# The first loads and a whole instruction order, in a kernel of sparse attention and a gated feed-forward layer

## The chip, the cores and the metric

One core of a Trainium2 chip. A core has five engines that run beside each other, each through its own instructions in order: TensorE (PE, matrix products; its weight loads are PEld), VectorE (DVE), ScalarE (ACT), GpSimd (POOL) and SyncE (SP), which here only issues transfers. ScalarE and GpSimd issue some too. Transfers run on 16 DMA engines that all queues share. The metric is the time of one execution on the device in microseconds (us); a profiled execution gives the time of every instruction.

## The reference

Attention over 4 batches of 8 heads, 768 positions of 64 values, with a mask by blocks of 32 (neighbours, the first and last block, three drawn blocks a row), and then a feed-forward layer with gate `h * sigmoid(beta * h)`:

```python
scores = scale * np.matmul(q, k.transpose(0, 1, 3, 2))
...
scores = np.where(mask, scores, -1000000000.0)
scores = scores - np.max(scores, axis=-1, keepdims=True)
attn = np.exp(scores)
attn = attn / (np.sum(attn, axis=-1, keepdims=True) + 1e-09)
...
h = x @ w_in                                  # 3072 x 512 by 512 x 2048
g = h * (1.0 / (1.0 + np.exp(-beta * h)))
return (g @ w_out).astype(np.float32)         # 2048 x 512
```

## The kernel before

The kernel writes its work as some 1,300 nodes: loads, casts, turns, score steps, exponentials, masks, attention products, projections, gates, output products. A node is a handful of instructions on one engine. The nodes are made by functions `add_...`, each with a model's duration, and then **emitted in the order of the table STEPS** (line 43, read by `in_steps`, line 164). A step such as `31S4` means node 31, on SyncE, in buffer 4; the letters P, A, D, G, S are the five engines. A step with a colon (`118P1:119`) is two matrix-product nodes whose products are split in two halves of 64 rows and interleaved, so that both halves of the array work; each such pair stands twice, once for either half (`in_halves`, line 321). A step such as `5x64V7` is five products of a zero tile, 64 columns wide, into bank 7, which compute nothing. What follows another in the table follows it in its engine's queue; the waits between engines come from the data.

**Heads in pairs.** 16 pairs of heads (4 batches of 4). A unit of attention is one pair and 256 or 512 query positions. For a unit, TensorE makes score steps of 1,024 columns (`sc`, eight or four products and, in the first six units, as many products that add the mask), ScalarE takes exponentials of them (`ex`, tile `et`, 128x1024), VectorE multiplies masks into the others (`mk`), TensorE multiplies by the values (`av`), VectorE normalizes (`norm`, tiles `recip` and `xst`). After 256 or 512 positions of all four pairs come 16 projections (`hp`), each followed by a tanh on ScalarE (tile `t_sb`) and a gate on VectorE (tile `g`); then output products, for six of the seven stretches by a scheme with seven instead of eight products that needs sums of weights (`w_mix`) and of gates (`s`) from VectorE.

**The start.** Queries and keys arrive as f32 with positions on partitions (tiles `st`, or `g` used as staging), are cast to f16 (tile `s`, s16 with its full name), turned by TensorE (`turn`, a product with `identity`) and copied out of PSUM into `kX` and `qX`. Pairs 0 and 1 get their keys in two loads (positions 0 to 255, and the rest), and their queries in two as well. `add_load` (line 502) puts a load on SyncE's queue, except those named in BESIDE (line 132), which `emit_first` (line 358) puts on ScalarE's queue before all else. The mask is built at the same time: a small product (`mt`), from it the fill for masked scores (tile `s`, 128x384, `neg`) and a copy (`mask_q`, `mtc`), then three products `km` with `onehot` and their copies into `mask01`. The weights are loaded by GpSimd's queue after the load named in GATE (line 131) has landed.

Of the kernel before, what the change touches and what calls it, by code (L numbers as in the profile page):

```python
# [43 lines left out]
31S4 0D 1P0 27S0 35S 32D0 33P4 28D1 45S1 13S1 29P7 17S3 21S 46G6 36D 18G2 30D0 3A 4P5 8P1 2A 41S0  # L44
6P0 7D 61S 42G3 51S2 62G5 37P3 52G4 55S3 34A 88P3 89Ab 69G 70G 38D 14D0 92P1 93A0 9D 47P1 15P0
19P4 22D 23P6 5A 16D2 24D 20D 71G 72G 73G 74G 75G 90P1 80P2 43P6 44D1 48A 91A2 76P1 10S 65S 63P0
64D 104P3 81A1 77A3 105A4 53P1 78P1 56D3 57P4 54D3 58D 79Ae 39S5 25S4 100P0 40D3 184P3 102P2 101A5
112P1 103A6 26D1 49S6 94P0 95P 113A7 82P2 83P 96D1 97D1 116P0 84Da 185A0 114P1 117Ac 190P3 66D0
85D0 191A8 59S7 60G2 50D0 106P2 107P 108Da 109D2 115Ab 188P0 86P6 67P7 189Ad 87D1 68D 186P2
118P1:119 202P3 119P 187A9 194P0 120Dh 121D3 203A1 192P2 11P2 110P3 98P6 122P7 12D 111D 193A4  # L50
195A2 204P1 123D 99D 205A3 124P5 145P4 125A2 139P7 142P0 133P6 146A0 143A3 134A1 136P2 127P1 140A5
130P3 126D0 147D 212P2 137A6 128A2 131A4 144D 135D 141D 213A5 138D 132D 206P3 207A6 151P2 157P3
163P4 154P5 158A0 164A1 129D 155A4 152A5 159D 210P3 196P0 211Ae 165D 156D 153D 208P2 228P1 197P
209Aa 198D0 220S4 221D5 199D3 169P6 229A7 166P7 223S8 170A0 160P4 148P5 167A6 161A3 149A2 234P1
168D 171D 150D 162D 224D1 214P0:215 235Ab 231P3 215P 232A0 243P2 172P23:178 216Df 217D2 244A8 245D
236D 230D 240P3 260P0 241A3 261A4 233D 242D 262D 272P2 178P 179P:173 263P3 273Ac 344D 274D 269P0
270A2 264Aa 173P 174P:180 345D 222S0 237P0 275P2 238A5 180P 266P3 175P 181P 265D 239D 271D 226S2
252S5 276Ad 225S 267A1 255S6 258S7 284S4 287S8 253G2 254S1 277D 246P3:247 396P2 176A1 397Ae 182A0
268D 279P0:278 247P 340D 341D 342D 256G6 387P2 248De 249D1 290S0 404S3 285G4 259G0 257S 286S3 183S
407S1 388A6 278P 384P1 385A9 250P6 200P4 218P7 280D2 281D4 201A2 251D 219D 282P5 381P0 382Ac 283D  # L60
390P1 393P3 310P4 394A5 292P1 391A8 293A0 313P7 295P0 314A2 343D 389D 386D 346D 311A4 296A3 395D
347D 392D 301P5 302A6 298P6 405G3 227G3 412P1 294D0 315D 312D 303D 299A5 325P17:307 418P2 410S5
413A0 300D 398D 297D 307P 415P1 408G0 288G5 289S 411G1 291G2 383D 419A2 308A5 309D 326A6 327D
304P6 305A1 316P0 416A3 317A2 319P7 320A0 306D 414D 318D 417D 321D 334P5 335A1 421P1 422A7 328P1
329A6 322P0 323A0 427P3 336D 348D0 330D 324D 331P23:337 428Ab 424P2 425A1 337P 400P0:399 435P3
399P 429D 420D 426D 423D 438P2 338A1 332A5 401D8 402D0 436A4 441P3 439Ae 333D 430P0:431 440D 339D
447P2 431P 442Ac 448Aa 437D 444P3 450P1 445A0 357P4 406S2 409S 470P3 354P5:358 451A1 464P1 471A5
358P 432D9 433D3 351D 458P0 461P3 465A8 467P1 459Ad 468A2 446D 452D 355P 449D 462A6 352D 443D 349D
453P0 454P 568P1 466D 356D0 359D 473P3 455Dc 456D1 569A9 365P:362 565P0 469D 474A3 472D 570D 460D
463D 475D 576P1 566Ae 362P 363P:366 577Aa 403S2 177S 590S4 593S1 591G2 601P3 562P0 602A7 366P 361D  # L70
477P1:476 364D 604P3 476P 360D 353D 563Ab 367A1 598P0 478D3 479D2 371P 605A0 350D 582P3 599A8
583A2 623P1 368P:372 624A6 620P0 626P3 372P 579P1 369P 596S5 434S 612S2 615S8 618S7 634S6 621A1
637S0 457S 640S3 578D 594D0 613D4 584D 567D 373D 592S0 480S 580A5 627A4 481P0 482A6 499P1 564D
625D 370D 638G5 616G6 635G2 487P2 500A0 595S 571P3 572P 488A1 483D1 501D 642P0 489D 614S2 656S4
659S1 374P3:490 484P24:496 600D 573D4 636S1 657G4 660G3 643A9 617S 658S3 639S 377S 661S 378S 645P0
646Ac 490P 491A5 606D 574D0 575S1 622D 644D 619D3 492D 581D 648P3 496P 649A3 485A1 486D 508P0
509A5 510D 493P1 520P3 497A6 521A0 494A2 375P 376A 502P0 628D 503A3 522D 498D 495D 504D 603D 529D0
670P1 664P3 671Ad 511P5 512A1 517P4 513D 607P1 608P 597G2 665Ab 666D 609D1 610D3 647D 518A6 681P0
682Ae 678P3 526P5 683D 585P1 586P 587D5 588D4 505P0 527A3 679A8 692P1 519D 528D 667P3 506A4 514P1
693A0 629P2 523P2 630P 515A0 507D 650D 516D 631D0 632D0 651P0:652 668A7 684P3 524A5 525D 652P  # L80
653Dc 685Aa 641G0 532D 654D2 790P2 791A1 535P23:538 698P3 796P0 538P 539P:536 802P2 672D 686D 530D
533D 797A6 699A2 536P 803A5 537A0 669D 680D 695P0 787P3 540D 673P2 674P 675Dc 676D1 543P 696Ac
788A7 810P2 799P0 662S2 688P3:687 546P:544 800Ab 663G1 798D 694D 531D 700D 633S 380S 379S 833S6
836S4 839S8 687P 813P0 689Df 690D0 544P 811Ad 841P2 847P3 814A4 655S 534D 589S 864S0 793P0 834G0
842A9 545A 547P 848A3 677S 691S 611S 697D 701P2 702P 542D 794A0 548A1 815D 703D0 704D2 549P 550P
801D 865D5 541D 551D 705S 844P3 825P0 822P2 823A8 826Aa 845Ae 552P 553P 555P 706P0 709P1 812D 795D
792D 789D 804D 554D 837G3 707A1 710A3 708D0 711D 730P3 819P2 731A2 806P3:805 824D 732D 843D 820A2
816P0 817Ac 805P 853P2 739P3:556 872P0 807D4 808D3 867S0 870S1 895S3 898S6 866S0 849D 818D 850P3
868G1 901S7 821D 556P 854A0 715P45:712 557D 851A5 740A3 856P3 873A1 857A6 871G2 896G2 741D 852D
874D 712P 716A2 717D 827D 713A1 835S2 558S 561S 721P23:727 878P0 875P3 879A7 727P 724P4 828P0 855D  # L90
714D 876Ab 722A6 858D 899G6 560S 838S 897S1 559S 809S0 900S 869S 728A3 725A4 742P5 751P7 718P6
743A0 877D 723D 829P 726D 729D 744D 830D1 881P1 831D2 719A5 752A3 745P45:733 846D 753D 882A2 884P0
733P 885A4 734A2 746A0 720D 736P23:748 987P0 754D0 735D 747D 988A8 748P 737A3 860P3:859 738D 749A6
984P0 887P2 859P 888Aa 750D 996P1 861D7 883D 862D0 760P45:763 985Ac 1038P0 990P3 763P 764P:761
997A5 991A0 886D 757D 880D 755D 889D 759D 1039Ad 1027P1 761P 890P0:891 1018P3 1028A3 762A1 758D
765D 891P 892D6 1019A9 893D1 768P:771 1021P1 993P3 1022A6 994Ae 1015P0 771P 772P:769 1007S1 1010S5
832S 1016A1 1030P1 999P3 863S 1000A2 1031A4 902G3 840D0 766D 1011D3 769P 894S 930P1 903P7 931A2
933P3 915P0 909P2 904A1 770A 756D 767D 998D 986D 1008D6 924P6 934A5 910A4 1009S3 1013S5 1012S
1001D 989D 995D 1017D 905D1 918P7 774P 932D 773A0 921P1 935D 1032D 911D 916A2 925A0 919A3 912P3
917D 992D 920D 775P 776D 926D 906P2 777P 922A6 923D 913A0 907A1 914D 908D 1014D1 1029D 1003P3:1002  # L100
1061P0 1062A7 780P:778 1047P1 1002P 1041P0 1004Dg 1005D0 778P 1048Aa 1166P1 1050P3 1042Ae 1167A0
1024P0 781P 936P2 1025Ac 1051A2 927P0 937A6 1040D 928A4 782A 779D 951D0 1020D 953D 1023D 952D
1043D 938D 948P7 942P6 949A2 943A5 929D 1026D 785S 786S 939P3 940A3 945P2 946A1 944D 950D 947D
941D 1044P2 1034P0:1033 1053P3 1033P 1035Da 1036D1 784S 1006S2 783S 1037S 1045Ab 1054A8 1076P2
1049D 957P23:960 1077A5 1064P3 1067P0 1052D 1065A9 1068A1 960P 961P:958 1055D 1046D 954D 955D
1073P2 958P 1180P3 1070P0 1074A3 959A1 1169P2 1069D 963D 1075D 962D 1066D 956D 965P 966P 1170A4
1071A6 1056P2 1057P 1072D 1208P0 1181Ac 1058Df 967A 968P:971 1059D0 1209Ae 1078D 1200P2 1201A2
1182D 1168D 1171D 1063D 1183P3 971P 972P:969 1184Aa 1060S 1194P0 1172P2 1173Ab 969P 1080P3:1079
1211P2 970A0 1210D 1185D 964D 973D 1195A8 1079P 1212Ad 1081D9 1082D4 977P:974 1213D 1214P0 1215A1
1186P2 1197P3 1187A6 974P 978P 1083P0 975P 1198A3 1084A 1216D 1217P2 1218P 979A 1188D 1219D3  # L110
1220D2 1115P2 1189P3 1091P0 1174D 1175P2 1176P 1190P 1085P1 1116A6 1086A3 976D 1202D 1199D 1177D7
1178D0 1196D 1097P3 1191Dc 1087D1 1127P4 1094P5 1192D4 1112P1 1128A3 1092A4 1129D 1095A0 1113A5
1093D 1117D 1114D 1203P3 1204P 1124P4 1125A5 1088P2 1205Dh 1206D3 1089A4 1103P7 1118P0 1221P6
1098A6 1104A2 1119A1 1126D 1090D 1096D 1099D 1105D 1121P4 1109P1 1122A0 1110A4 1106P2 1107A2 982S
1179S1 980S 1123D 1120D 981S 1193S 983S 1130P5 1131A3 1222D 1111D 1132D 1207S 1108D 1247P6 1100P7
# [16 lines left out]
BESIDE = (("k", 1, 0), ("k", 0, 0))  # L132
# [962 lines left out]
```

## Time and profile before

| | us |
|---|---|
| median of 3 runs (lowest, highest) | 261.37 (261.06, 262.38) |
| the profiled execution | 261.5 |
| its span, first to last instruction | 259.7 |
| PE, DVE, ACT, POOL busy | 252.3, 220.1, 212.5, 37.8 |

The busy times are shares of one span and overlap. A stage is read by the engine that is full in it, and the chain of work that ended last says which engine's delay would have moved the end. Lines of instructions all read L199, since a helper records them; they are told apart by tiles. Tile names stand without their buffer numbers in the profile.

### The profile page before, as it was taken

To read this page: it belongs to the slowest core of one execution; us is meant where nothing else is said; L and a number is where in the kernel's file an instruction comes from. 1 tells how busy PE (TensorE), PEld (TensorE's weight loads), DVE (VectorE), ACT (ScalarE), POOL (GpSimd) and SP (SyncE) were. 2 spreads that over 40 slices of the span, in tenths; PEclk is the share of its full clock that TensorE was granted. 3 is DMA by queue.
4 is the path that set the end of the run, shared out by engine and by line. 5 is a ranking of instruction groups with operands and counts; after the bars stand their busy time and mean duration, and the time that the engine had idled before them with its cause. 6 is when DMAs were issued, how large, how long until landed. Compare 5 with 4: busy or idle time off the path is not lost.

```text
span 259.7 us, 8901 instructions
## 1 busy us (share of the span) xinstructions
PE 252.3 (97%) x3823; PEld 171.9 (66%) x3823; DVE 220.1 (85%) x430; ACT 212.5 (82%) x287; POOL 37.8 (15%) x52
## 2 busy tenths in 40 slices
PE   5999999999999999999999999999999999999995
PEld 1576675554367866558776457846758986568884
DVE  4465548999999999999999999998999967889572
ACT  3599999899999997999988989885999892866051
POOL 4661000133400106011201410010000000000000
PEclk9999999999999999999999999999999999999999
DMA  6999999694429997734949785232051101400042
GB/s 194 371 280 225 243 190 223 222 238 129 91 70 263 285 144 194 182 62 142 237 121 257 215 120 144 25 55 67 5 175 31 23 5 53 143 0 3 0 162 83
DMA packets 49883, 36.83 MB, mean 142 GB/s; under 512 B 29732, under 2 KB 46388, under 8 KB 49844
## 3 DMA queue, kind: packets, MB, share of 16 engines
q1 hardware_dynamic: 45584, 31.80, 49.1%
q0 software_dynamic: 3680, 4.19, 9.4%
q8 instruction: 30, 0.49, 0.7%
q10 hardware_dynamic: 580, 0.26, 0.4%
q14 instruction: 9, 0.07, 0.1%
HBM read 27.27 MB, written 6.29 MB: 129 GB/s over the span
## 4 chain that ended last, share of the span: by engine, by line
PE 78%; DVE 16%; ACT 2%; DMA 2%; issue 1%; ACTq 0%; DVEq 0%
PE sc L199 78%; DVE et L199 7%; DVE g L199 5%; DMA st<-in_k_dram 2%; DVE w_mix L199 1%; ACT et L199 1%; ACT t_sb L199 1%; DVE xst L199 1%; DVE w_out_sb L199 0%; DVE s L199 0%; DVE osb L199 0%; DVE x L199 0%; DVE recip L199 0%; ACTq L362 0%; DVEq L199 0%
## 5 line engine op out<-in xcount | busy, mean ns | idle before, releaser
L199 ACT ACTIVATE et<-sc 128x1024 f16<-128x1024 f32 x144 | 139.0, 1037 | 12.6 <-PE sc L199 11.6
L199 PE MATMUL sc<-x,w_in_sb 128*128 128x512 f16 (+2 forms) x512 | 91.9, 352 | 0.1
L199 ACT ACTIVATE t_sb<-sc,beta_c_sb 128x512 f16<-128x512 f32 (+1 forms) x112 | 65.0, 646 | 20.5 <-PE sc L199 17.2
L199 DVE TENSOR_TENSOR et<-et,mask 128x960 f16<-128x960 f16 x120 | 77.5, 679 | 1.3 <-ACT et L199 1.3
L199 DVE SCALAR_TENSOR_TENSOR g<-t_sb,sc 128x512 f16<-128x512 f16 (+1 forms) x112 | 63.5, 604 | 10.0 <-ACT t_sb L199 9.8
L199 PEld LDWEIGHTS <-w_in_sb 128*128 128x128 f16 (+1 forms) x512 | 43.0, 97 | 36.3 <-issue 3.5
L199 PEld LDWEIGHTS <-g 64*128 64x128 f16 (+1 forms) x700 | 49.0, 96 | 15.0 <-issue 2.6
L199 PE MATMUL sc<-w_out_sb,g 64*128 64x256 f16 (+3 forms) x568 | 55.5, 281 | 0.0
L199 PE MATMUL sc<-qX,kX 64*128 64x512 f16 (+1 forms) x384 | 51.0, 329 | 0.6 <-ACT et L199 0.3
L199 PEld LDWEIGHTS <-et 64*128 64x128 f16 (+1 forms) x1800 | 41.4, 95 | 9.4 <-issue 2.3
L199 PE MATMUL sc<-va,et 64*128 64x65 f16 (+1 forms) x1800 | 44.5, 191 | 0.1
L199 POOL CAST s<-st 128x768 f16<-128x768 f32 (+2 forms) x19 | 18.1, 967 | 83.3 <-DVE et L199 60.3
L199 PEld LDWEIGHTS <-kX 64*128 64x128 f16 x384 | 20.1, 96 | 10.3 <-issue 5.5
L199 PEld LDWEIGHTS <-s 64*128 64x128 f16 (+1 forms) x320 | 21.8, 98 | 6.9 <-DVE s L199 2.0
L199 PE MATMUL sc<-w_mix,s 64*128 64x256 f16 (+1 forms) x272 | 23.7, 270 | 0.0
L199 ACT COPY osb<-sc 128x512 f32<-128x512 f32 (+3 forms) x23 | 12.4, 539 | 8.3 <-PE sc L199 7.3
L199 DVE TENSOR_TENSOR xst<-sc,recip 128x256 f16<-128x256 f32 (+1 forms) x32 | 17.8, 556 | 0.9
L199 DVE TENSOR_TENSOR osb<-osb,sc 128x512 f32<-128x512 f32 (+2 forms) x19 | 11.7, 616 | 7.0 <-PE sc L199 2.7
L199 PE MATMUL sc<-w_mix,g 64*128 64x256 f16 (+3 forms) x128 | 15.3, 264 | 0.0
L199 POOL CAST va<-st 128x768 f16<-128x768 f32 x9 | 8.6, 962 | 39.5 <-PE sc L199 33.0
L199 DVE RECIPROCAL recip<-sc 128x4 f32<-128x4 f32 (+1 forms) x32 | 6.1, 191 | 8.2 <-PE sc L199 7.9
L199 PE MATMUL sc<-s,onehot 64*128 64x256 f16 (+1 forms) x72 | 11.7, 338 | 0.2
(61 smaller groups left out, 95.6 us busy)
## 6 DMA issues: line engine op xcount, KB each, us to landing
out_dram<-osb SPq DMA_DIRECT2D x23, 256.0 KB, 2.4
st<-in_k_dram SPq DMA_DIRECT2D x12, 384.0 KB, 5.0
st<-in_q_dram SPq DMA_DIRECT2D x12, 384.0 KB, 4.8
st<-in_v_dram SPq DMA_DIRECT2D x12, 384.0 KB, 4.6
g<-in_v_dram SPq DMA_DIRECT2D x4, 384.0 KB, 6.5
w_in_sb<-in_moe_w_in_dram POOLq DMA_DIRECT2D x2, 512.0 KB, 8.1
w_in_sb<-in_moe_w_in_dram POOLq DMA_DIRECT2D x1, 1024.0 KB, 14.5
w_out_sb<-in_moe_w_out_dram POOLq DMA_DIRECT2D x2, 512.0 KB, 18.4
```

The source lines that it names most:

```text
L199: r = f(*a, **kw)
```

## The change

Three things change in the code: which loads are on ScalarE's queue, two durations and a dependency of the mask in the model, and the whole table STEPS, which was made anew with a model that has TensorE wait at every 256th instruction. The program has no such wait; it is a number in the model that orders it.

```diff
-31S4 0D 1P0 27S0 35S 32D0 33P4 28D1 45S1 13S1 29P7 17S3 21S 46G6 36D 18G2 30D0 3A 4P5 8P1 2A 41S0
-6P0 7D 61S 42G3 51S2 62G5 37P3 52G4 55S3 34A 88P3 89Ab 69G 70G 38D 14D0 92P1 93A0 9D 47P1 15P0
+13S1 17S3 14G1 5x64V7 0D 1P0 2A 31S4 27S0 35S 32D3 33P2 21S 41S0 28D2 29P1 30D1 45S1 34A 36G 18D6
+3A 1V7 22D 51S2 88P2 61S 15P0 19P2 37P1 38D 23P7 42G1 16A0 20A 24D 46D0 89A6 76P1 52G2 77A9 92P0
...
-BESIDE = (("k", 1, 0), ("k", 0, 0))
+BESIDE = (("k", 0, 0), ("q", 0, 0))
...
-        n_mb = add("mask", "DVE", 980, 90, mb, at=2240.0)
+        n_mb = add("mask", "DVE", 860, 90, mb, at=2600.0)
...
-        n_mtc = add("mask", ("ACT", "DVE"), COPY384, 100, mtc, deps=[n_mt], use=[tb])
+        n_mtc = add("mask", ("ACT", "DVE"), COPY384, 100, mtc, deps=[n_mt, n_neg[-1]], use=[tb])
```

All kinds of work keep their counts. 47 pairs of halves stand in the table instead of 44, TensorE gets one zero product of 512 columns and five of 64 more, 27 nodes change their engine, among them three more casts on GpSimd than before and three fewer on VectorE, and two output copies that go from ScalarE to VectorE.

**The first loads, SyncE's queue.** `st_4` holds pair 1's queries, `st_0` its keys; `st_1` and `st_3` are pair 0's keys and queries; `g` stages pairs 2 and 3. Before:

```order
L509 DMA st_4_134<-in_q_dram 128x2x128
L509 DMA st_0_130<-in_k_dram 128x2x256
L509 DMA g_0_110<-in_q_dram 128x2x384
L509 DMA st_3_133<-in_q_dram 128x2x128
L509 DMA st_1_131<-in_k_dram 128x2x256
L509 DMA g_0_110<-in_k_dram 128x2x384
```

After, the same queue:

```order
L509 DMA st_4_134<-in_q_dram 128x2x128
L509 DMA st_0_130<-in_k_dram 128x2x128
L509 DMA st_0_130<-in_k_dram 128x2x256
L509 DMA st_1_131<-in_k_dram 128x2x256
L509 DMA g_0_110<-in_k_dram 128x2x384
L509 DMA g_0_110<-in_q_dram 128x2x384
```

Both short loads of pair 1 now lead this queue; pair 0's rest of keys has moved ahead of the loads of pairs 2 and 3.

**ScalarE's queue at the start.** `kX_0`, `qX_0` are pair 1's before and pair 0's after, `kX_1`, `qX_1` the other way round; `s_0_117` is the fill for masked scores. Before:

```order
L509 DMA st_0_130<-in_k_dram 128x2x128
L509 DMA st_1_131<-in_k_dram 128x2x128
L199 ACT_TABLE_LOAD
L199 CAST mask_q_155<-sc_0_61 24x384
L199 ACTIVATE s_0_117<-sc_0_61 128x384
L199 COPY qX_0_123<-sc_2_63 128x256
L199 ACTIVATE et_11_76<-sc_3_64 128x1024
L199 ACTIVATE et_0_65<-sc_1_62 128x1024
L199 CAST mask01_156<-sc_2_63 128x384
L199 COPY qX_1_125<-sc_0_61 128x768
```

After:

```order
L509 DMA st_1_131<-in_k_dram 128x2x128
L509 DMA st_3_133<-in_q_dram 128x2x128
L199 ACT_TABLE_LOAD
L199 ACTIVATE s_0_117<-sc_0_61 128x384
L199 COPY qX_1_125<-sc_1_62 128x256
L199 CAST mask_q_155<-sc_0_61 24x384
L199 COPY kX_0_122<-sc_0_61 128x256
L199 COPY qX_0_123<-sc_1_62 128x256
L199 ACTIVATE et_6_71<-sc_2_63 128x1024
L199 ACTIVATE et_9_74<-sc_1_62 128x1024
```

Two copies of pair 0 now stand ahead of the first exponential, and a copy of 768 columns and one of the mask no longer stand behind the second. On TensorE, the three products `km` with `mask_q`, which stood ahead of the first scores, come only after the sixth and the seventh score step.

**VectorE in the middle, between two normalizations.** `et` are exponentials that get the mask, `w_mix` sums of weights, `s16` a cast of a later pair's loads. Before, up to the second normalization:

```order
L199 TENSOR_TENSOR et_10_75<-et_10_75,mask01_156 128x8x120
L199 TENSOR_TENSOR et_5_70<-et_5_70,mask01_156 128x8x120
L199 TENSOR_TENSOR et_2_67<-et_2_67,mask01_156 128x8x120
L199 TENSOR_TENSOR et_13_78<-et_13_78,mask01_156 128x8x120
L199 TENSOR_TENSOR et_1_66<-et_1_66,mask01_156 128x8x120
L199 TENSOR_TENSOR w_mix_150<-w_out_sb_149 128x1024
L199 TENSOR_TENSOR w_mix_150<-w_out_sb_149,w_mix_150 128x1024 x2
L199 RECIPROCAL recip_14_99<-sc_3_64 128x8
```

After:

```order
L199 TENSOR_TENSOR et_13_78<-et_13_78,mask01_156 128x8x120
L199 TENSOR_TENSOR et_10_75<-et_10_75,mask01_156 128x8x120
L199 TENSOR_TENSOR et_9_74<-et_9_74,mask01_156 128x8x120
L199 TENSOR_TENSOR et_14_79<-et_14_79,mask01_156 128x8x120
L199 TENSOR_TENSOR et_2_67<-et_2_67,mask01_156 128x8x120
L199 CAST s16_4_143<-st_3_133 128x2x6x64
L199 TENSOR_TENSOR et_0_65<-et_0_65,mask01_156 128x8x120
L199 TENSOR_TENSOR w_mix_150<-w_out_sb_149,w_mix_150 128x1024
L199 RECIPROCAL recip_14_99<-sc_3_64 128x8
```

A cast that GpSimd had now stands among VectorE's masks, and two of the weight sums stand earlier or later than they did.

More of the change, by code (lines that the diff above doesn't have):

```diff
@@ L49 @@
[L49 to L60, printed above, removed]
@@ L124 @@
+1238P1 1259P0 1148P 1255D 1149D 1150P 1151P 1153P 1256P5 1239A0 1152A1 1146D 1156P 1154P 1157P
+1262P3 1241P7 1260A6 1266A4 1257A1 1261D 1242A2 1263A6 1155D 1267D 1250P0 1247P4 1251A5 1248A3
+1158D 1162S 1240D 1243D 1264D 1258D 1252D 1249D 1271D0 1274D 1276D 1163S 1275D 1272D 1159P 1160P
+1161A 1165S 1164S 1277P1 1279P5 1278A0 1283P 1284A 1280D 1285P 1286A1 1281D 1282D 1273D 1287P
+1288D 1289P 1297S 1290D 1296S 1291A 1292P 1293A 1294P7 1295D 1298S
 """
```

139 lines of the change are left out of this document (73 added, 66 removed).

## The prediction

> **What bounds the kernel now.** I read the page first, then busy time by stage, then the chain of work that ended last, then the first 14 us instruction by instruction, then single transfers.
>
> ```profile
> span 259.7 us, 8901 instructions
> PE 252.3 (97%) x3823; PEld 171.9 (66%) x3823; DVE 220.1 (85%) x430; ACT 212.5 (82%) x287; POOL 37.8 (15%) x52
> ```
>
> TensorE (PE) is busy for 97% of the span. A share over the whole says little, so the stages come next: columns are the stretch, its length, then busy us (and instructions) of PE, weight loads, VectorE (DVE), ScalarE (ACT) and GpSimd (POOL), the clock, DMA share and GB/s.
>
> ```profile
> 13.00:41.00 28.00, 27.81 (x485) 19.76 (x485) 16.66 (x44) 28.00 (x41) 5.48 (x7) 1.00 1.17 231
> 41.00:75.00 34.00, 33.44 (x512) 17.05 (x510) 33.41 (x59) 32.51 (x44) 9.10 (x10) 1.00 0.63 162
> 75.00:200.00 125.00, 124.57 (x2067) 85.46 (x2060) 119.42 (x212) 112.24 (x141) 16.41 (x16) 1.00 0.64 145
> ```
>
> From 13 to 41 us ScalarE has no idle time at all (28.00 of 28.00) and TensorE hardly any; from 41 to 75 VectorE is full (33.41 of 34); after that TensorE (124.57 of 125). The chain agrees (start, length, what):
>
> ```profile
> 1.43 3.90 DMA st<-in_k_dram
> ...
> 5.70 14.01 PE sc L199 x177
> ...
> 42.09 2.94 DVE et L199 x6
> ...
> 73.86 0.70 DVE xst L199
> ...
> 199.71 56.82 PE sc L199 x710
> ```
>
> The chain begins with a load on ScalarE's queue, the first part of pair 1's keys. VectorE holds it at both ends of the middle stretch; the last 57 us are TensorE alone. So a gain at the start is worth something if ScalarE and TensorE both carry it to 41 us, and if VectorE's work from there to 74 us does not grow. Nothing after 75 us gives a gain by itself unless TensorE works less.
>
> **The change part by part.** All moves at the start are read from this stretch (start, duration, engine, operation, idle time before it and what ended that):
>
> ```profile
> 0.74 0.46 SPq L509 DMA_DIRECT2D st<-in_q_dram  x1
> ...
> 1.25 0.46 SPq L509 DMA_DIRECT2D st<-in_k_dram  x1
> ...
> 1.43 0.92 ACTq L509 DMA_DIRECT2D st<-in_k_dram  x2
> ...
> 4.81 0.35 ACT L199 COPY qX<-sc 128x256 f16<-128x256 f16 x1
> 5.36 0.63 DVE L199 CAST s<-st 128x256 f16<-128x256 f32 x2 [1.69 <-DMA st<-in_k_dram]
> ...
> 5.70 0.40 PE L199 MATMUL sc<-identity,s 128*128 128x128 f16 x2 [1.36 <-DVE s L199]
> ...
> 6.03 1.14 PE L199 MATMUL sc<-mask_q,onehot 24*128 24x384 f16 x3
> 6.14 0.29 DVE L199 COPY kX<-sc 128x256 f16<-128x256 f16 x1 [0.16 <-PE sc L199]
> ...
> 7.10 0.61 PE L199 MATMUL sc<-identity,s 128*128 128x128 f16 x4
> ...
> 8.25 0.42 PE L199 MATMUL sc<-qX,kX 64*128 64x256 f16 x2
> ...
> 8.72 1.94 ACT L199 ACTIVATE et<-sc 128x1024 f16<-128x1024 f32 x2 [3.56 <-PE sc L199]
> ...
> 10.54 0.48 ACT L199 CAST mask<-sc 128x384 f16<-128x384 f32 x1
> ...
> 10.90 0.83 ACT L199 COPY qX<-sc 128x768 f16<-128x768 f16 x1
> ...
> 12.14 16.68 ACT L199 ACTIVATE et<-sc 128x1024 f16<-128x1024 f32 x18 [0.41 <-PE sc L199]
> ...
> 13.43 0.27 PE L199 MATMUL sc<-qX,kX 64*128 64x256 f16 x2
> ```
>
> ScalarE waits 3.56 us for its first exponential at 8.72, because TensorE does the mask products (1.14) and the turns of the rest of pair 1's keys (0.61) before the first scores. One score step is four pairs at 0.21 us from start to start, about 0.85 us, as long as a pair shows 0.42; at 13.43 a pair shows 0.27 and starts are 0.11 apart. TensorE thus runs at half rate until about 12.8 us.
>
> *Loads.* Landing times are read from these transfers (KB of one, median us from issue to landing) and the rate:
>
> ```profile
> st<-in_q_dram SPq DMA_DIRECT2D x1, 128.0 KB, 2.2
> st<-in_k_dram ACTq DMA_DIRECT2D x1, 128.0 KB, 3.9
> st<-in_k_dram ACTq DMA_DIRECT2D x2, 128.0 KB, 4.5
> 3.00:4.00 1.00, 0.56 (x3) 0.16 (x3) 0.63 (x3) 0.66 (x1) 0.71 (x2) 1.00 0.98 292
> 4.00:5.00 1.00, 0.34 (x3) 0.07 (x2) 0.00 (x0) 0.95 (x3) 0.00 (x0) 1.00 1.04 315
> ```
>
> Pair 1's first keys go from ScalarE's queue (1.43 + 3.9 = 5.3) to the second place of SyncE's. With 2.2 us they would land at 3.5, with 3.9 at 5.2. I take 4.2: the load ahead of them lands at 0.74 + 2.2 = 3.0, and 256 KB more (they and ScalarE's first load beside them) at about 300 GB/s are 0.9 us, plus some lag. Pair 0's keys, now first on ScalarE's queue, land by the same count at about 4.3 (5.3 at worst). Pair 0's queries, second there, would land at 1.9 + 5.1 = 7.0 as the second one does now (median 4.5 of two, the first 3.9); the transfers they now share with are smaller (128 and 256 KB against 384), which gives about 5.5. I take 5.9, nearer to the count than to the old row since the bytes ahead are fewer. SyncE's queue carries no more bytes up to the gate load than before, so the weight loads' gate stays.
>
> *TensorE and ScalarE.* One more 512-column zero product and five 64-column ones stand where TensorE waits (1.36 idle before 5.70), so cost nothing; if that cover were gone, 0.5 us. Pair 1's key cast 4.2 to 4.5, two turns to 4.9, copy of 0.29 to 5.25, scores 5.35 to 6.2. But ScalarE is strictly in order, and ahead of the first exponential now stand both copies of pair 0 (keys and queries, 0.35 each). Queries: land 5.9, cast 6.2, turn 6.5, then the copy waits behind pair 0's key copy; it ends near 7.4. With semaphores the first exponential starts at 7.6, 1.1 us earlier than 8.72. Scores follow at half rate, 0.85 each: pair 0's first step 7.6 to 8.45, two steps of pair 1 to 10.15, twelve turns of 0.1 us (two took 0.40, four 0.61) to 11.35, then steps to 12.2 and 12.95. Exponentials at 16.68/18 = 0.93 us: four back to back from 7.6 to 11.45, a gap of 0.85, two more from 12.3 to 14.15. The sixth ends now at 12.14 + 4 x 0.93 = 15.85, so ScalarE is 1.7 ahead, less a mask copy (0.48) that now comes after it: **1.2**. (Its 0.83 copy of 10.90 is in that difference: it goes to VectorE.) TensorE at 12.95 has done two more score steps (0.87 at full rate) and six more turns (0.4), and lacks the three mask products (0.48): **0.8 ahead**. Both engines are full from 13 to 41, so I take **-1.1**, nearer to ScalarE's, the one without any idle time.
>
> *VectorE's stretch.* One cast of a later pair leaves GpSimd and stands among the masks of VectorE's full stretch.
>
> ```profile
> L199 DVE CAST s<-st 128x768 f16<-128x768 f32 x7 | 3.7, 545 | 0.0
> 49.20 1.13 POOL L199 CAST s<-st 128x768 f16<-128x768 f32 x1 [27.40 <-DVE et L199]
> ```
>
> The rows give 0.55 us on VectorE, and nothing on GpSimd, which had waited 27 us. Between the normalizations before and after it, one weight difference leaves and one mask multiplication comes in, which cancel by 75 us. VectorE has no room there: **+0.55**. At least 0 (if it fell in a wait), at most 1.1 (if a mask behind it makes TensorE wait as long again).
>
> *More halves.* 47 pairs of half-row products stand instead of 44, and 96 more products of 65 columns. Weight loads of one attention product:
>
> ```profile
> 34.18 0.81 PEld L199 LDWEIGHTS <-et 128*128 128x128 f16 x24 [0.42 <-issue]
> ...
> 39.84 0.81 PEld L199 LDWEIGHTS <-et 64*128 64x128 f16 x48 [0.20 <-POOLq L336]
> ```
>
> 24 whole ones and 48 halves take the same 0.81: **0**, within 0.1 either way. Casts of values that move to GpSimd and output copies that move from ScalarE to VectorE, all after 90 us: **0**, hidden by TensorE; bare, they would be about 1 us. The tail is laid out as before. The copy that reads the mask now waits for the fill before it, both on ScalarE in that order: 0.
>
> *Weight loads.* GpSimd now issues the second weight load after two value casts.
>
> ```profile
> 12.62 2.41 POOL L482 DMA_DIRECT2D w_in_sb<-in_moe_w_in_dram x3 [0.31 <-POOL w_in_sb L491]
> w_in_sb<-in_moe_w_in_dram POOLq DMA_DIRECT2D x1, 1024.0 KB, 14.5
> ```
>
> The third lands at 14.3 + 14.5 = 28.8 now and 1.5 to 2 us later if issue sets it, not at all later if the DMA engines do (share 1.17 from 13 to 41). I take 0, since the engines are full; the late end is a rival.
>
> Sum: -1.1 + 0.55 = -0.55. The profiled execution took 261.5 us (259.7 span and 1.8 around it), 0.1 above the median 261.37, so 261.4 - 0.55 = **260.8**.
>
> [...] The row of 13.43 against 8.25 shows one step up near 12.8, after seven us of nearly unbroken work. [...]
>
> **Rivals.** [...]
>
> [...]
>
> *C, the lead is lost before 41 us* (weights up to 2 us later, or VectorE's stretch starting by what it waits for): no gain, cast stays: 261.9. For it: ScalarE's stretch ends in projections which need those weights. Against it: full DMA engines set that landing.
>
> **How the numbers follow.** Forecast 0.43 (259.8 to 261.9, the ends of its terms), A 0.24, B 0.16, C 0.17. About 0.5% is what a measurement of this kernel can tell from no change: 260.1 to 262.7. Faster: most of A (0.2) and the low end of the forecast (0.1); slower: most of B (0.13), and 0.08 of C and the forecast for waits that a whole new order can bring after 75 us, where TensorE has 0.43 us of slack. Same: 0.49. The range 259.0 to 263.0 leaves out the far side of A and of B.
>
> **What would show it.** Right: pair 1's key cast near 4.2, first exponential near 7.6, ScalarE without a gap from about 12.2, VectorE full until about 73.5 and TensorE's last product near 255.8. Wrong if the first cast still waits past 5, if products stay 0.21 apart after 13 us, if VectorE idles between 42 and 74, or if TensorE's idle time after 75 us grows by over 1 us.

## The result

The changed kernel took 262.96 us (median of 18 runs, 260.74 to 264.51), the kernel before 261.57 us (18 runs, 260.32 to 262.84): a ratio of **1.0053**, with a 95% interval of 1.0031 to 1.0076. It is slower, by 1.4 us. The profiled execution took 262.87 us, with a span of 261.1, so that it stands for the median.

The page of the kernel after, its busy row, and the windows that answer to those shown of before:

```profile
span 261.1 us, 9103 instructions
PE 251.7 (96%) x3921; PEld 173.6 (67%) x3921; DVE 218.1 (84%) x429; ACT 211.0 (81%) x285; POOL 38.2 (15%) x55
```

```profile
13.00:41.00 28.00, 26.96 (x579) 18.82 (x574) 15.46 (x43) 26.86 (x40) 7.64 (x10) 1.00 1.18 237
41.00:75.00 34.00, 32.31 (x490) 17.25 (x488) 31.88 (x59) 31.49 (x42) 7.64 (x9) 1.00 0.69 158
75.00:200.00 125.00, 123.82 (x2036) 85.47 (x2037) 117.16 (x210) 111.68 (x139) 17.28 (x18) 1.00 0.60 144
```

No engine is full in its stretch any more. ScalarE idles 1.14 us between 13 and 41, VectorE 2.12 between 41 and 75, TensorE 1.18 after that, where it idled 0.43 before.

The start itself came out as meant. From its timeline (the first cast of pair 1's keys, score products, and ScalarE's first exponential):

```profile
4.71 0.29 DVE L199 CAST s<-st 128x256 f16<-128x256 f32 x1 [1.18 <-DMA st<-in_k_dram]
...
6.42 0.42 PE L199 MATMUL sc<-qX,kX 64*128 64x256 f16 x2
...
7.74 1.04 ACT L199 ACTIVATE et<-sc 128x1024 f16<-128x1024 f32 x1
...
8.17 0.28 PE L199 MATMUL sc<-s,onehot 64*128 64x256 f16 x2
...
8.29 0.27 PE L199 MATMUL sc<-qX,kX 64*128 64x256 f16 x2
```

The first exponential starts at 7.74 instead of 8.72, and a pair of products takes 0.27 to 0.28 us from 8.17 on: the clock stepped up near 8.1 us, not near 12.8 (the traces' clock records have 8.12 and 12.78). So the lead at the start was larger than forecast. The chain of work that ended last shows where it went:

```profile
20.30 0.51 issue
20.81 0.04 POOLq L199
20.85 0.86 POOL w_out_sb L485
21.71 0.62 POOL s L199
22.33 0.78 POOL va L199
23.15 28.05 PE sc L199 x536
51.20 1.20 issue
...
53.42 0.70 DVE xst L199
...
74.24 0.70 DVE xst L199
...
126.25 5.58 DMA out_dram<-osb
131.93 0.59 ACT osb L199
...
200.73 57.16 PE sc L199 x707
```

Three places are new: GpSimd's queue holds TensorE near 22 us, TensorE waits 1.20 us at 51.20 for nothing that the profile shows ("issue"), and ScalarE waits near 126 to 132 for a store to land, so that its tile can be written again. Two normalizations can be set against the chain of before: 53.04 and 73.86 there, 53.42 and 74.24 here. By the starts of ScalarE's activations, counted from the first exponential (tanhs included), and the last product of TensorE, both counted from the two traces:

| | before | after | lead of after |
|---|---|---|---|
| 7th activation | 15.82 | 13.36 | 2.46 |
| 16th | 24.05 | 22.68 | 1.37 |
| 17th | 24.96 | 24.61 | 0.35 |
| 49th | 45.75 | 45.20 | 0.55 |
| 55th | 53.75 | 54.15 | -0.40 |
| 133rd | 121.15 | 121.60 | -0.45 |
| 144th | 134.37 | 135.14 | -0.77 |
| TensorE's last product | 256.32 | 257.69 | -1.37 |

A lead of 1.0 us goes at 23 to 24.6 us, another 0.95 at 51, and about 0.6 near 133, since the chain's last long piece of TensorE starts at 200.73 instead of 199.71, 1.02 us behind. The last 0.35 go after 200 us. Near 132 the rows are these:

```profile
131.93 0.59 ACT L199 COPY osb<-sc 128x512 f32<-128x512 f32 x1 [1.30 <-DMA out_dram<-osb]
133.50 0.61 PE L199 MATMUL sc<-qX,kX 64*128 64x512 f16 x4 [0.55 <-ACT et L199]
134.41 0.39 PE L199 MATMUL sc<-qX,kX 64*128 64x512 f16 x2 [0.31 <-ACT et L199]
```

### The profile page after: what moved, and what is told of

The parts are those of the page before. It is cut to its first block, busy times and chain, and to the rows that moved or that the text cites. A ratio compares the mean times of both kernels' runs of the same rounds, so it can differ in the third digit from the quotient of the medians.

```text
span 261.1 us, 9103 instructions
## 1 busy us (share of the span) xinstructions
PE 251.7 (96%) x3921; PEld 173.6 (67%) x3921; DVE 218.1 (84%) x429; ACT 211.0 (81%) x285; POOL 38.2 (15%) x55
## 4 chain that ended last, share of the span: by engine, by line
PE 87%; DMA 5%; ACT 2%; DVE 2%; SPq 1%; issue 1%; POOL 1%; POOLq 0%; ACTq 0%; DVEq 0%
PE sc L199 87%; DMA g<-in_q_dram 2%; DMA out_dram<-osb 2%; ACT et L199 1%; SPq L509 1%; ACT t_sb L199 1%; SPq L747 1%; DVE xst L199 1%; DVE g L199 0%; ACT osb L199 0%; POOL w_out_sb L485 0%; POOL va L199 0%; POOL s L199 0%; DVE s L199 0%; DVE recip L199 0%
## 5 line engine op out<-in xcount | busy, mean ns | idle before, releaser
L199 ACT ACTIVATE et<-sc 128x1024 f16<-128x1024 f32 x144 | 138.9, 1037 | 11.4 <-PE sc L199 8.0
L199 PE MATMUL sc<-x,w_in_sb 128*128 128x512 f16 (+2 forms) x508 | 91.1, 352 | 0.0
L199 ACT ACTIVATE t_sb<-sc,beta_c_sb 128x512 f16<-128x512 f32 (+1 forms) x112 | 64.4, 632 | 21.1 <-PE sc L199 20.1
L199 DVE TENSOR_TENSOR et<-et,mask 128x960 f16<-128x960 f16 x120 | 75.4, 667 | 0.8 <-ACT et L199 0.8
L199 DVE SCALAR_TENSOR_TENSOR g<-t_sb,sc 128x512 f16<-128x512 f16 (+1 forms) x112 | 63.6, 605 | 10.0 <-ACT t_sb L199 9.8
L199 PEld LDWEIGHTS <-w_in_sb 128*128 128x128 f16 (+1 forms) x508 | 42.4, 97 | 36.9 <-issue 3.5
L199 PEld LDWEIGHTS <-g 64*128 64x128 f16 (+1 forms) x706 | 50.0, 96 | 14.0 <-issue 3.4
L199 PE MATMUL sc<-w_out_sb,g 64*128 64x256 f16 (+2 forms) x576 | 56.3, 282 | 0.2
L199 PE MATMUL sc<-qX,kX 64*128 64x256 f16 (+1 forms) x384 | 50.6, 325 | 1.2 <-ACT et L199 1.2
L199 PEld LDWEIGHTS <-et 64*128 64x128 f16 (+1 forms) x1896 | 42.1, 95 | 9.8 <-issue 2.7
L199 PE MATMUL sc<-va,et 64*128 64x65 f16 (+1 forms) x1896 | 44.7, 191 | 2.2 <-issue 1.6
L199 POOL CAST s<-st 128x768 f16<-128x768 f32 (+2 forms) x20 | 18.2, 923 | 114.7 <-DVE g L199 43.2
L199 PEld LDWEIGHTS <-kX 64*128 64x128 f16 x384 | 19.8, 94 | 11.5 <-issue 6.7
L199 PEld LDWEIGHTS <-s 64*128 64x128 f16 (+1 forms) x320 | 21.7, 97 | 6.3 <-DVE s L199 1.9
L199 PE MATMUL sc<-w_mix,s 64*128 64x256 f16 (+1 forms) x272 | 23.8, 270 | 0.1
L199 ACT COPY osb<-sc 128x512 f32<-128x512 f32 (+3 forms) x21 | 11.2, 543 | 9.8 <-PE sc L199 7.4
L199 DVE TENSOR_TENSOR xst<-sc,recip 128x256 f16<-128x256 f32 (+1 forms) x32 | 17.8, 557 | 1.2 <-DVE recip L199 0.3
L199 DVE TENSOR_TENSOR osb<-osb,sc 128x512 f32<-128x512 f32 (+2 forms) x19 | 11.7, 617 | 7.9 <-PE sc L199 5.2
L199 DVE RECIPROCAL recip<-sc 128x4 f32<-128x4 f32 (+1 forms) x32 | 6.2, 194 | 11.7 <-PE sc L199 9.0
L199 PE MATMUL sc<-w_mix,g 128*128 128x256 f16 (+3 forms) x120 | 14.2, 264 | 0.0
L199 POOL CAST va<-st 128x768 f16<-128x768 f32 x10 | 8.5, 871 | 19.7 <-PE sc L199 8.5
L199 PE MATMUL sc<-s,onehot 64*128 64x256 f16 (+1 forms) x72 | 10.7, 315 | 0.2 <-DVE xst L199 0.2
```

The costliest lines, as they stand in the source:

```text
L199: r = f(*a, **kw)
```

## The experiments

The theory to be tested: **the new start is a gain, and three places of the new order give it back** (near 22, 51 and 132 us). The rivals: a lead is worth nothing here because later engines are full; the cast that moved to VectorE costs 0.55 us; the larger number of TensorE's instructions costs time by itself.

### The start alone

The first 82 steps of the new table (with its BESIDE), the six weight loads in one row behind their gate, then the old order without the steps already done. Two casts stay on VectorE and three `et` buffers have other numbers. The edit, against the kernel after:

```diff
-69G 70G 25S4 39S5 91A5 79A1 26G0 10S 49S6 65S 81A2 40G1 71G 56D1
+69G 70G 71G 72G 73G 74G 75G 25S4 39S5 91A5 79A1 10S 49S6 65S 81A2 56D1
...
+104P0 105A4 5D 58D 9D 40D3 184P3 102P2 112P1 103A7 26D1 94P0 95P
```

> The first 82 steps of the new table (through about 14.7 us, with the weight loads issued in one row and two value casts left on VectorE as in the old one), then the old order. Give-back theory (the new start is a real gain, later places of the new order give it back): TensorE 1.3 to 1.6 us ahead of the old kernel at 15 us and still 0.8 or more ahead at 41; the time 0.6 to 1.2 us under the kernel before. Rival (a lead of TensorE is worth nothing here, since VectorE is full from 41 to 74 us and sets the end of that stretch): the lead is gone by 75 us, the time within 0.3 us of the kernel before.

> The same kernel as the new start with the old order, a second time. Give-back theory: 0.3 to 0.8 us under the kernel before, TensorE 0.5 to 1.0 us ahead at the end. Rival (no gain): within 0.2 us.

It took 261.09 us beside 261.55 (ratio 0.9993, 0.9972 to 1.0014) and, a second time, 261.11 beside 261.49 (0.9988, 0.9974 to 1.0002): about 0.4 us under the kernel before, less than the first theory's 0.6 to 1.2, and neither interval excludes equality. From the first profile, two normalizations of its chain and ScalarE's exponentials near 35 us; the third fence has those of the kernel before:

```profile
52.14 0.70 DVE xst L199
...
72.96 0.70 DVE xst L199
```

```profile
32.88 1.18 ACT L199 ACTIVATE et<-sc 128x1024 f16<-128x1024 f32 x1
35.02 1.94 ACT L199 ACTIVATE et<-sc 128x1024 f16<-128x1024 f32 x2 [0.96 <-PE sc L199]
```

```profile
34.73 3.07 ACT L199 ACTIVATE et<-sc 128x1024 f16<-128x1024 f32 x3
```

VectorE's stretch runs 0.9 us earlier from end to end, so a lead that reaches 41 us is not lost to full engines: that rival falls. But half of the lead goes just before. ScalarE is still 1.85 us ahead at 32.88, then waits 0.96 us, and is 0.84 ahead at 35.02 (this exponential is at 35.86 in the kernel before). The second profile has the same wait of 0.96 us (at 35.83) and goes from 1.04 us ahead to 0.03; its normalizations come only 0.1 us early (52.94 and 73.76).

The wait belongs to the way this kernel was put together. The exponential of 35.02 (node 209) writes buffer a of `et`. One of the three renumbered buffers is that of node 191 (`191Aa`, in the old order `191A8`), and the value products that read the tile of node 191 run from 34.12 to 35.05. In the old order no exponential before node 209 writes buffer a. So the 0.4 us may be less than the start is worth; no run here has the start without this wait, and the two kernels below that use this start have it too. The landing of the weights took nothing that shows: TensorE waits 0.48 us for them in the first profile (at 29.96) and not in the second, and ScalarE's lead is the same 1.85 us before and after.

### The cast on VectorE

The kernel before with one letter changed, the cast of 49.2 us.

```diff
-287S8 253G2 254S1
+287S8 253D2 254S1
```

> The kernel before with one change: the cast of 49.2 us (values' partner keys of a later pair) on VectorE instead of GpSimd, as the new kernel has it. The prediction's step (VectorE is full from 41 to 75 us, so a cast more lengthens the time): VectorE's normalization near 73.9 us comes 0.55 us later and the time is 0.4 to 0.6 us over the kernel before. Rival (VectorE fills that stretch because it waits for little else, and TensorE's products bind there): under 0.2 us.

261.15 us beside 261.55, ratio 0.9985 (0.9967 to 1.0004): no cost shows, against the 0.4 to 0.6 us of the prediction's step. Its chain shows why (before had "47.37 3.47 DVE et L199 x5" in the same place):

```profile
47.54 1.71 DVE et L199 x3
49.25 0.47 DVE s L199
49.72 1.14 DVE et L199 x2
...
73.88 0.70 DVE xst L199
```

Five masks and the cast take 3.32 us here, and five masks without the cast took 3.47 in the kernel before, where the cast ran on GpSimd from 49.20 to 50.33. Four of those five took 0.65 us each, and the one that began beside the cast took twice as long, until 0.5 us after the cast's end:

```profile
49.58 1.25 DVE L199 TENSOR_TENSOR et<-et,mask 128x960 f16<-128x960 f16 x1
```

So the cast on GpSimd cost VectorE 0.6 us, about what it costs on VectorE itself (0.47 in the chain). The whole trace of the kernel before has the same pattern: of its 120 masks, the 103 with no cast of GpSimd beside them take 0.61 to 0.66 us, and the nine that begin during a cast take 0.68 to 1.28 and end 0.51 us after that cast's end.

### GpSimd's queue near 22 us

Rows of the kernel after for GpSimd and for ScalarE's next exponential:

```profile
17.27 0.74 POOL L482 DMA_DIRECT2D w_in_sb<-in_moe_w_in_dram  x1 [1.14 <-PE sc L199]
18.00 1.50 POOL L485 DMA_DIRECT2D w_out_sb<-in_moe_w_out_dram  x2
20.82 0.89 POOL L485 DMA_DIRECT2D w_out_sb<-in_moe_w_out_dram  x1 [1.32 <-PE sc L199]
21.70 0.63 POOL L199 CAST s<-st 128x512 f16<-128x512 f32 x1
22.25 0.84 POOL L199 CAST va<-g 128x768 f16<-128x768 f32 x1
```

```profile
24.61 1.94 ACT L199 ACTIVATE et<-sc 128x1024 f16<-128x1024 f32 x2 [0.89 <-PE sc L199]
```

GpSimd's weight loads wait twice for TensorE. That is the note that closes the first pass of a pair of halves: `one.met = two.met = nc.gpsimd.nop().ins` in `in_halves` stands in GpSimd's queue, waits for the halves, and the second pass waits for it. Behind the last weight load stands the cast of pair 1's remaining queries (node 66), which was VectorE's before; its turn, copy and score step release the exponential of 24.61. Three kernels try this place.

All loads in one row, the two first value casts on VectorE:

```diff
-69G 70G 25S4
+69G 70G 71G 72G 73G 74G 75G 25S4
...
-26G0
-40G1
+54D3 64D 26D0
+5D 58D 40D1 9D
```

> The new kernel with GpSimd's six weight loads in one row after their gate, as before, and the two first value casts on VectorE. Give-back theory: the 1.25 us that TensorE loses between 20 and 25 us shrink to 0.3; TensorE's lead over the old kernel at 25 us is 1.0 or more instead of 0.1. The wait of 1.2 us near 51 us stays, so that the time falls by 0.3 to 1.0 us against the new kernel. Rival (the loss there is from the longer mask work that the new order puts behind the first scores): the loss between 20 and 25 us stays above 0.9 us.

263.73 us, ratio 1.0098 (1.0078 to 1.0118): a miss, and an edit with a fault of its own. On VectorE the casts stand ahead of the mask copy:

```profile
15.02 0.55 DVE L199 CAST va<-g 128x768 f16<-128x768 f32 x1
15.49 0.55 DVE L199 CAST mask<-sc 128x384 f16<-128x384 f32 x1
```

TensorE waited 0.40 us before 16.09 for that copy, and node 66 still stood behind the notes (21.33). So a cast that is moved also has to be followed on the queue that it goes to.

Node 66 alone, ahead of the last four weight loads:

```diff
-112P2 94P 72G 73G
+112P2 94P 66G2 72G 73G
...
-75G 66G2 60G3
+75G 60G3
```

> The new kernel with one cast of GpSimd (the remaining queries of pair 1) moved ahead of the last four weight loads and of the pair of halves whose end GpSimd's queue waits for. Chain theory (ScalarE's 0.89 us without work before 24.61 us comes from this cast: weight load, cast, turn, copy, score step): ScalarE has no wait over 0.3 us between 20 and 30 us, the 17th activation starts by 23.8 instead of 24.61, TensorE's lead over the old kernel at 25 us is 0.8 or more instead of 0.1. The waits near 51 and 132 us stay, so the time falls by 0 to 0.9 us only. Rival (VectorE's reciprocals and copies bind there): the 17th activation stays after 24.3.

263.64 us, ratio 1.0075 (1.0049 to 1.0101). The step itself went nearly as the chain said (23.87 for "by 23.8", a wait of 0.47 for "under 0.3"), the time did not fall:

```profile
23.87 2.86 ACT L199 ACTIVATE et<-sc 128x1024 f16<-128x1024 f32 x3 [0.47 <-PE sc L199]
```

```profile
31.02 1.05 PE L199 MATMUL sc<-x,w_in_sb 128*128 128x256 f16 x8 [1.38 <-DMA w_in_sb<-in_moe_w_in_dram]
```

The 17th activation starts 0.74 us earlier, and six us later TensorE waits 1.38 us for the third part of the weights. Behind the first bound stands a second one, the landing of the weights. That profile also has waits at two of the borders told of below, 0.60 us before 52.51 and 0.97 before 90.59.

The four early pairs of halves as whole products, which takes the notes away:

```diff
-83P1:82 184P2 102P3 185A7 95P0:94 82P 112P2 94P
+82P1 184P2 102P3 185A7 94P0 83P 112P2 95P
...
-107P3:106 106P
+106P3 107P
...
-119P2:118
+118P2
...
-118P
+119P
```

> The new kernel with the four pairs of halves between 14 and 25 us as whole products, 192 instructions of TensorE fewer there; each whole product beside score products costs up to 0.2 us by the all-whole kernels, 0.4 to 0.8 in sum. If the early pairs carry the loss: GpSimd's weight loads follow each other without waiting for TensorE, ScalarE has no wait over 0.3 us between 20 and 25 us, no wait at a block border before 30 us, and the time is 0.3 us or more under the new kernel (262.96). If they do not: 0.3 us or more over it.

261.88 us, ratio 1.0026 (1.0008 to 1.0043): 1.1 us under the new kernel by the medians, though the interval overlaps with that of the new kernel's first measurement (1.0031 to 1.0076). GpSimd's queue runs through:

```profile
14.93 1.48 POOL L482 DMA_DIRECT2D w_in_sb<-in_moe_w_in_dram  x2
16.40 2.38 POOL L485 DMA_DIRECT2D w_out_sb<-in_moe_w_out_dram  x3
18.95 0.61 POOL L199 CAST s<-st 128x512 f16<-128x512 f32 x1 [0.17 <-issue]
```

Weights and node 66 are both early now, and the 17th activation starts at 23.64. This kernel also shifts everything later by 192 instructions of TensorE, which moves the waits of the next part (its chain has 0.23 us at 43.7, 0.28 at 53.7 and 0.52 at 92.4, instead of 1.20 at 51.2 and 0.16 at 89.5), so the 1.1 us are not this place's alone.

### The wait at 51 us

TensorE of the kernel after, the row of its page for instruction packets, and the busy share of the DMA engines from 46 to 52 us:

```profile
49.33 1.86 PE L199 MATMUL sc<-va,et 64*128 64x65 f16 x107
52.39 0.78 PE L199 MATMUL sc<-va,et 64*128 64x65 f16 x39 [1.20 <-issue]
```

```profile
q8 instruction: 30, 0.49, 0.8%
```

```profile
DMA  9999999999999999999999999999899910003999
```

The queue called "instruction" moves 30 packets of 16 KB in the whole execution. TensorE's trace has 7,863 records (3,921 products, as many weight loads, 21 of its sequencer), so a packet is some 256 of them. Counted in the trace, 1729 = 6 x 256 + 193 records stand ahead of the wait. Two others of the kind, 0.26 us at 17.74 and 0.16 at 89.50, have 449 = 256 + 193 and 3009 = 11 x 256 + 193 records ahead of them, and one of 0.06 us in the kernel before has 2753 = 10 x 256 + 193. Call such places borders. The n-th packet belongs to the n-th border: at the seven borders up to 52 us of the kernel after it begins 2.4 to 4.3 us after TensorE crosses it. For the border at 46.96 it began at 49.70, beside loads that keep the DMA engines full until 51, took 1.06 us, and TensorE went on 1.64 us after its end; the two shorter waits ended 1.41 and 1.42 us after the end of theirs. The block in between is dense (107 value products in 1.86 us, by the row) and was crossed in 4.04 us, less than its successor took to come.

Three loads moved behind the transposes of 50 us:

```diff
-255S5 258S0 284S6 287S1 290S8 256G1 254S0 385A8
+255S5 258S0 256G1 254S0 284S6 287S1 290S8 385A8
```

> The new kernel with three loads (pair 6's keys, queries and values, 384 KB each) moved from 42 to 44 us on SyncE's queue to behind the transposes of 50 us. Theory that TensorE's wait of 1.2 us at 51.2 is for its next 256 instructions, whose fetch stood behind the loads: the fetch begins within 1.8 us instead of 2.7 us of the crossing, the wait falls under 0.3 us, and the time falls by 0.5 to 1.1 us. Rival (the wait has another cause than the load on the DMA engines): the wait stays above 1.0 us.

262.78 us, ratio 1.0065 (1.004 to 1.0089). TensorE from 49.5 us, and the transfers from 46 to 52:

```profile
49.51 3.20 PE L199 MATMUL sc<-va,et 64*128 64x65 f16 x192
```

```profile
DMA  9999999999999000000000000000000000000299
```

192 products follow each other without a wait; the packet began 0.78 us after the crossing. At 52.24 the normalization is 1.2 us earlier than in the kernel after. Yet no gain in time is shown (262.78 against 262.96 by the medians, where 0.5 to 1.1 was forecast): ScalarE then waits 1.8 instead of 1.3 us for the store near 132, and TensorE's last product comes 0.3 us earlier.

The first pair of halves whole, 48 instructions fewer ahead of this place:

```diff
-83P1:82
+82P1
...
-82P
+83P
```

> The new kernel with the first pair of halves as whole products, which gives TensorE 48 instructions fewer ahead of everything later and the same work. Theory that the wait at 51 us is for the next 256 instructions: it moves 48 instructions (24 value products) further on, and since that block of 256 is crossed in 2.0 us instead of 4.05, it grows to 1.2 to 2.2 us. Rival (it waits for data of that product): it stays at the same product, 1.0 to 1.4 us.

262.57 us in one run. Its products before and after the wait:

```profile
49.58 2.24 PE L199 MATMUL sc<-va,et 64*128 64x65 f16 x131
52.29 1.13 PE L199 MATMUL sc<-va,et 64*128 64x65 f16 x61 [0.48 <-issue]
```

131 products instead of 107 run before it: the wait moved by 24 products, which are 48 instructions, and again has 1729 records ahead of it. It is no wait for data of a product. Its size was a miss: 0.48 by this row, not 1.2 to 2.2, since the border before it now falls at 49.61, where the packet began after 0.26 us.

The new kernel itself once more:

> The new kernel itself, a second execution with a profile. Fetch theory: ScalarE's wait before 24.6 us and the waits near 51 and 132 us (the two together 1.0 us or more) are there again, and the waits at block borders near 17.5 and 89 us lie anywhere between 0 and 1.1 us; time 1.0 to 1.8 us over the kernel before. Rival (the wait near 51 us was an accident of one execution): it is under 0.3 us.

263.69 us beside 261.40, ratio 1.0092 (1.0061 to 1.0124). The waits at 51 and 132 are there again: 0.95 us before 52.38, 1.3 of ScalarE for the store. At the border near 17.8 us hardly any is left (0.02), near 89.5 it is 0.44. Over the kernels of this study the wait near 89 us lies between 0 and 1.05 us, the longest with the old order behind the new start, and the same kernel had 0.16 and 0.44: it differs from execution to execution. The ratio itself was 1.0053 at the first measurement, so gains against the new kernel of some tenths of a microsecond are not told by one run.

### The store at 132 us, and both together

One store moved ahead of the loads:

```diff
-800Ab 833S0 540D
+800Ab 378S 833S0 540D
...
-814A0 378S 677S
+814A0 677S
```

> The new kernel with one output store moved ahead of the five loads and three transposes that precede it on SyncE's queue near 120 us. Give-back theory: ScalarE no longer waits 1.30 us for that store's tile at 131.9, TensorE's two waits of 0.71 and 0.47 us near 133 shrink to under 0.3 together, and the time falls by 0.7 to 1.0 us against the new kernel. Rival (TensorE has slack there, the waits come back at the next place): the waits go, the time falls by under 0.3 us.

262.66 us, ratio 1.004 (1.002 to 1.006). In its profile ScalarE waits for no store (TensorE's two waits, 0.55 and 0.31 us by the rows shown with the result, are gone too) and TensorE's last product starts 1.5 us earlier (256.17); 0.4 of that is there before the store already (the 133rd activation at 121.19). That execution took 261.33 us, at the low end of its runs (260.9 to 263.5). By the medians the gain is 0.3, the rival's size. Why the runs without a profile show so little of it stays open.

> The new kernel with three loads moved behind the transposes of 50 us and one output store moved ahead of the loads near 120 us; the cast of GpSimd stays where the new kernel has it. If the waits near 51 and 132 us carry the loss: neither is there, TensorE's last product comes near 255.8 instead of 257.7, and the time is 261.0 to 261.7. If the waits at block borders come elsewhere in most executions: the profile may show the gain, the time stays over 262.2.

With both of these moves: 261.58 us beside 261.49, ratio 1.0011 (0.9992 to 1.003). That is 1.4 us under the new kernel's 262.96 and level with the kernel before. The two hide each other in part: without the wait at 51 us ScalarE reaches the store earlier (133rd activation at 120.76 instead of 121.60) and waits there for longer, 1.8 us.

> The new kernel with three moves at once: that cast of GpSimd early, three loads behind the transposes of 50 us, and one output store ahead of the loads near 120 us. Give-back theory: the waits near 22, 51 and 132 us are all gone, their sum is 0.9 + 1.1 + 1.0 = 3.0 us less what full engines take back (0.3 to 1.0), so the last product of TensorE comes 2.0 to 2.7 us earlier than in the new kernel (255.0 to 255.7) and the time is 260.2 to 261.0, 0.5 to 1.3 us under the kernel before. Rival (other waits take their place): the time is not under that of the kernel before.

With node 66 early as well: 262.54 us (1.0027, 1.0 to 1.0055), a miss. In its profile TensorE's weight loads wait 1.1 us for the weights near 31 us, as in the kernel with that cast alone, and TensorE waits 1.04 us at a border before 25.15.

> Both of these. If both places carry it: 260.5 to 261.3, under the kernel before. If only the later two: 261.3 to 262.2, as the loads and the store alone give less the cost of whole products. If neither: over 262.5.

The early pairs whole and both moves: 261.73 us (1.0008, 0.9989 to 1.0027), which fits "only the later two". The gains do not add: the early pairs gave 1.1 us by themselves, the two moves 1.4, all together 1.2. So how much each place carries stays open.

### Whole products everywhere

All pairs of halves undone (47 in the new table, 44 in the old, each as above), which leaves TensorE some 5,630 instructions.

> The new kernel with all 47 pairs of halves as whole products: the same sums in the same places, TensorE's instructions fall from about 7,840 to 5,630, and the notes between TensorE and GpSimd that close a pair go. Fetch theory (the new order loses about 1 us more than the old one in TensorE's waits for its next 256 instructions, because it crosses blocks of 256 faster while loads fill the DMA engines): TensorE's waits at block borders fall from 2.1 us to under 0.4 in sum, GpSimd issues the last weight load 1 us or more earlier, the wait of ScalarE before 24.6 us shrinks, and the time falls by 1.0 to 2.0 us against the new kernel (262.96), to 261.0 to 262.0. Rival (more instructions cost nothing, the loss is in the order of the work): within 0.4 us of the new kernel.

> The kernel before with all 44 pairs of halves as whole products. Fetch theory: its profile shows only 0.2 us of such waits, so the time moves by -0.5 to +0.2 us; what halves are worth by themselves shows here. Rival (halves are worth something to TensorE, for instance in weight loads): the time rises by 0.5 us or more.

> The new kernel with whole products, with three loads moved behind the transposes of 50 us and one output store moved ahead of the loads near 120 us. Fetch and store theories together: no wait over 0.3 us at a block border, none near 132 us; 0.5 to 1.0 us under the whole products alone, and under the kernel before (260.2 to 261.2). Rival: another place takes the gain, and the time stays over 261.5.

> The new start with the old order behind it, all products whole. Give-back theory: the lead of 1.5 us at 15 us is kept to about 0.7 at the end, and with 0.4 us less of waits at block borders the time is 0.6 to 1.2 us under the kernel before (260.4 to 261.0). Rival: the old order has no waits to lose there, so that the time is that of the new start alone (261.1).

They took 269.69 (ratio 1.0327, 1.0305 to 1.0349), 270.40 (1.0345, 1.0326 to 1.0364), 269.29 (1.03, 1.0283 to 1.0317) and 269.53 us (1.0314, 1.0295 to 1.0332). Every forecast with an upper end was wrong by some 8 us; the two rivals that gave only a lower end (0.5 us or more over the kernel before, and over 261.5 us) held. A pair of halves saves about 0.2 us in the old order (8.9 us over 44 pairs) and 0.14 in the new one (6.7 us over 47), where the waits at borders go at the same time. Why a whole product costs more was not shown. What the four runs still tell: without halves, and so without waits at borders (none over 0.12 us in the profiles of the first two) and without the notes on GpSimd's queue, the new order is not the slower one, 269.69 against 270.40.

### A version under both

The start alone and the cast on VectorE, the two parts of the change that did not slow the old kernel:

> The new start with the old order, and the cast of 49 us on VectorE. If both are worth what they showed alone (0.4 us each): 260.5 to 261.0, under the kernel before by more than its interval. If either was chance: 260.9 to 261.6.

260.96 us beside 261.40, ratio 0.9984 (0.9971 to 0.9997): the only kernel of this study that is faster than the kernel before by more than its interval, though barely. The two gains do not add up, and 260.96 lies in both forecasts.

## Why the prediction was wrong

Forecast was 0.55 us less, measured 1.4 more. The step that failed is the zeros of the sum: for casts that move to GpSimd, for more halves and for all the rest of the new order the prediction put nothing, and there the runs show about 1.8 us, of which the waits at 51 and 132 us carry most. That 262.96 still lies inside the range (259.0 to 263.0) is luck: the upper end was there for B, a clock that steps up later than at 12.8, and for C (261.9), and the clock stepped up early. No run shows the size of the shift that A (a clock that steps up earlier, 0.24), B (0.16) and with them the ends of the range stand for; it was the author's estimate. What the profiles showed with the new start is a clock that stepped up anywhere from 4.8 to 11.0 us. By the prediction's own steps:

- **Loads, first exponential: right.** The first cast came at 4.71 (forecast 4.2), and pair 0's copies, the last of them at 7.48, set the first exponential at 7.74 (7.6), as forecast.
- **The start lead of -1.1: too small as a lead, too large as a gain.** The forecast left the clock's step at 12.8 us; it came near 8.1, and ScalarE's 7th activation came 2.46 us earlier. But the start alone, with the old order behind it, gave 0.4 us. What took the rest there was a wait of 0.96 us for a buffer that the kernel of that run brought with it, and neither reason of rival C: ScalarE's lead outlived the landing of the weights, and VectorE's stretch carried what was left. What the start is worth without that wait was not measured.
- **"One cast ... +0.55": fell.** By itself it measured no cost (0.4 us under the kernel before, within the noise). The prediction asked whether VectorE had room for the cast and not what GpSimd's cast did to VectorE's mask beside it, 0.6 us.
- **"Casts of values that move to GpSimd ..., all after 90 us: 0": the step that failed first.** Three casts of pairs 0 and 1 move to GpSimd before 25 us; two of them the prediction itself names under weight loads. The third, of queries, behind weight loads that wait for TensorE's halves, takes back 1.0 us at 24.6.
- **"More halves: 0": read from weight loads alone.** By the kernels of whole products a pair of halves saves 0.14 to 0.2 us, so three pairs more would save 0.4 to 0.6 (an estimate, not measured). And a pair also puts a note into GpSimd's queue, and every instruction of TensorE counts toward the next block of 256. A row that pointed there was on the page of before, the 30 packets of instructions.
- **"Nothing after 75 us gives a gain by itself", and 0.08 for waits there: too little.** The store at 132 us lies there, and at 51 us, in the stretch that the prediction read by VectorE alone, TensorE waited for instructions. Taking both away gave 1.4 us, the whole difference, though making the early pairs whole gave 1.1 without either move.

So the forecast -0.55 becomes, by what was measured: -0.4 for the start in the old order, 0 for the cast, and about +1.8 for what the new order adds to it (262.96 less 261.1). Of that, 1.4 are the two waits together by the run that takes both away. How the rest splits between 22 us and the pieces after 200 us was not settled; if the start is worth more than 0.4, the rest is larger.

## What to carry to other kernels

When a whole order is made anew, the places that the change is about are a small part of what moves: walk every engine's queue for instructions that change engine, for buffers that wait for a store, and for loads that now stand beside a dense stretch. Count TensorE's instructions in blocks of 256: the blocks that ended in a wait here were crossed in 2 to 6 us while loads filled the DMA engines. A bound that is taken away uncovers the next one: here GpSimd's cast hid the landing of weights, and the instruction wait hid part of the wait for the store. And a kernel that is put together from two orders can bring a wait of its own, so read its profile for buffers before its time is taken as the worth of a part.

## What was not expected of the hardware

- **Waits for instructions.** In the kernel after TensorE stood 0.26, 1.20 and 0.16 us at three of its 30 borders, each with 256k + 193 records of its trace ahead of it, where loads were in flight and the block short: the blocks ahead of the three were crossed in 5.5, 4.0 and 5.5 us at a DMA share of 1.13, 1.01 and 0.93. Two blocks that were crossed faster, in 3.4 and 3.8 us at a share of 0.17 and 0.21 (to 76.5 and 197.5 us), end without a wait of TensorE's products. So the wait at every 256th instruction, which the change calls a number in the model, stands in the trace too, though not at every border and not of one size: at 51 us it was 0 with the loads moved.
- **A cast on GpSimd cost VectorE half of its length** where VectorE multiplied masks beside it: 3.47 us for five masks with a cast of 1.13 us beside them, 2.85 (1.71 + 1.14) without. All of it fell on the one mask that began during the cast.
- **The step of the clock** came near 8.1 us in the kernel after, and anywhere from 4.8 to 11.0 in the 17 profiles of kernels with that start (11.6 to 12.8 in the three with the old one). By the clock records the stretch at full clock lasted 245.76 us in the kernel before and 252.59 in the kernel after. What sets the moment of the step was not shown. The 7th activation moved with it only between 12.7 and 14.2 us.
